# Linear attention and a highway layer on one core: half-height turns of k and q, row-halved scores and state, a compact state, and a new written order

## The chip, the core and the metric

The kernel runs on one core of a Trainium2 chip. The metric is the device time of one execution in microseconds. Three runs of the kernel before gave 109.04, 109.41 and 110.59; the median is 109.41.

## What is computed

First a decayed causal attention in blocks of 64 rows, with a 64 by 64 state for each batch and head; then a highway layer on the result.

```python
# q, k, v: (4, 8, 768, 64); lam: one decay for each of 8 heads
for b in range(768 // 64):
    intra = einsum('bhic,bhjc->bhij', qb, kb) * Dmask        # lam ** (i - j) for i >= j
    intra = einsum('bhij,bhjd->bhid', intra, vb)
    inter = einsum('bhid,bhde->bhie', qb * lam_pow, kv_state)
    out[:, :, sl] = intra + inter
    kv_state = lam_block * kv_state + einsum('bhsd,bhse->bhde', kb * rev_pow, vb)

x = out.transpose(0, 2, 1, 3).reshape(3072, 512)
H = maximum(x @ w_h, 0)
T = 1 / (1 + exp(-(x @ w_t + b_t)))
return T * H + (1 - T) * x                                   # (3072, 512), float32
```

## The kernel before

**Tiling.** The sequence is cut into twelve chunks of 256 rows, three for each batch, numbered n = 0 to 11. A chunk has two blocks b of 128 rows. Two consecutive rows lie in one partition (J = 2, the index j), so a load (`load`, line 170) moves runs of 512 bytes. The powers of the decay are put into q (`cast_q`, the factor `pow_q`) and v (`cast_v`, `pow_v`), both by `scale` (line 188), so that the mask is a triangle of ones and the state only adds up within a batch. k is only cast to bf16 (`cast_k`). Eight heads are four pairs hp of two heads e; in a transposed tile head e lies in the partitions `half(e)`.

**Stages of one chunk.** Tokens of the plan name them.

- `Lk Lq Lv`: loads of k, q and v, in halves of four heads (256 KB each), issued by SP. `CK CQ CV`: casts and scalings.
- `TK TQ`: transposes of k and q on PE (`trans`, line 199, into PSUM), eight 128x128 matmuls against the identity each. `EK EQ`: copies into `kT` and `qT` (lines 206 and 210).
- `SS.n.e` (`scores_state`, line 224): 16 score tiles of head half e (64 rows by 64 columns of the array, 128 columns moved), interleaved with 16 state tiles (64 columns moved) of block 1 - e. Scores of half e use the rows `half(e)` of the array, the states of block b the rows `half(b)`. The last chunk of a batch leaves out the state of block 1. Chunk 0 uses `S` and `U` instead.
- `KE` (`evac_s`, line 251): the PSUM state `kv` [128, 4, 128], which holds the two heads of a pair on its diagonal, is copied to `ss`. `M` (line 254): a mask of a PSUM bank of scores, 128x512, on DVE.
- `I` (`inter`, line 265): four 128x128 matmuls for a block, `ss` against `qT`. `A` (`intra`, line 276): 64x64 tiles, masked scores against `vs`, added in the same bank. `D` (`take`): copy to `xT`.
- `F.i.u.w` (`block`, line 295): eight matmuls of the highway layer for group i, column half u, weight w. `H` relu and subtraction on DVE (line 303), `G` two sigmoids on ACT (line 308), `X` the gate product (line 316), `R` (`turns`, line 340) the turn back, in half-height tiles of 64 rows against 64 columns of the identity, `E` its copy, `ST` the store by SP (512 KB). The last chunk is handled as two groups of 128 rows (11 and 12), with 128-column matmuls and stores in three parts.
- `W` loads a piece of the weights (512 KB, 256 rows of one matrix), `WC` casts a quarter matrix row block. `Z.r` runs r idle matmuls (`spin`) on PE.

**What sets the order.** The text `PLAN` (lines 17 to 60) is run from left to right (line 384). A token gives the operation, its indices, after `@` the engine, after `=` the PSUM banks (0 to 6; `kv` has one for itself). Each engine and each DMA queue works through its own instructions in this order; all large transfers are on SP's queue. SBUF buffers turn round in pools, five deep for the loads (`BUFS`, line 62).

Of the kernel before, what the change touches and what calls it, by code (L numbers as in the profile page):

```python
# [17 lines left out]
Lk.0.0 Lv.0.1 Lv.0.0 Lq.0.0 Lk.0.1 Lq.0.1 Lv.1.1 CK.0.0@POOL Lq.1.0 Z.12=0 TK.0.0=0 Lq.1.1 CV.0.0@DVE Lk.1.0  # L18
CQ.0.0@POOL EK.0.0@DVE Lv.1.0 CV.0.1@DVE CK.0.1@ACT Lk.1.1 Z.11=1 TQ.0.0=1 B=2 EQ.0.0@ACT CQ.0.1@POOL W.0.1 W.0.0
Z.6=0 TQ.0.1=3 TK.0.1=4 EQ.0.1@DVE U.0.0 EK.0.1@ACT W.1.1 S.0.0=56 KE.0.0@DVE S.0.1=01 CQ.1.2@POOL W.1.0 M.0.0.1 Z.1=3  # L20
U.0.1 I.0=34 M.0.1.1 KE.0.1@ACT Lk.2.1 M.0.0.0 A.0.1 M.0.1.0 TQ.1.2=0 Lq.2.1 CV.1.2@DVE CK.1.2@ACT EQ.1.2@ACT Lq.2.0
Z.8=1 TK.1.2=1 A.0.0 EK.1.2@DVE Lk.2.0 D.0.0@DVE Z.3=5 SS.1.1=56 WC.0.0.1@ACT WC.0.0.0@POOL M.1.1.0 KE.1.0@ACT
WC.0.1.0@POOL D.0.1@ACT Lv.2.1 WC.0.1.1@DVE Z.4=0 SS.1.0=01 M.1.1.1 I.1=35 KE.1.1@ACT Lv.2.0 F.0.0.0=4 WC.1.1.0@DVE PT
M.1.0.1 Lk.3.1 F.0.1.0=6 M.1.0.0 WC.1.0.0@POOL WC.1.0.1@ACT Lk.3.0 WC.1.1.1@DVE A.1.1 A.1.0 BC F.0.0.1=1 H.0.1 Lq.3.1
D.1.1@ACT H.0.0 D.1.0@ACT F.0.1.1=0 Lq.3.0 CQ.2.2@POOL F.1.0.0=2 Lv.3.0 G.0.1@ACT CK.2.2@DVE F.1.0.1=6 Lv.3.1
G.0.0@ACT X.0.1@DVE TQ.2.2=5 Lq.4.0 X.0.0@DVE TK.2.2=4 EQ.2.2@ACT CV.2.2@POOL F.1.1.0=3 Lq.4.1 EK.2.2@DVE G.1.0@ACT
H.1.0 SS.2.0=01 Lk.4.1 H.1.1 CK.3.2@POOL SS.2.1=54 Lk.4.0 M.2.0.1 F.1.1.1=2 KE.2.0@ACT M.2.1.0 Lv.4.0 TK.3.2=3 M.2.1.1
CQ.3.2@POOL G.1.1@ACT I.2=15 M.2.0.0 Lv.4.1 A.2.1 X.1.0@DVE A.2.0 Lk.5.0 R.0=40 D.2.0@ACT D.2.1@DVE CV.3.2@POOL
TQ.3.2=6 E.0.0@ACT Lk.5.1 F.2.1.1=1 E.0.1@ACT EQ.3.2@DVE Lq.5.1 EK.3.2@ACT X.1.1@DVE F.2.1.0=5 CQ.4.2@POOL Lq.5.0
R.1=40 H.2.1 SS.3.1=62 Lv.5.0 F.2.0.0=3 CK.4.2@POOL KE.3.0@ACT M.3.1.1 Lv.5.1 E.1.1@ACT M.3.1.0 SS.3.0=52 E.1.0@ACT  # L30
H.2.0 Lq.6.0 TQ.4.2=0 KE.3.1@ACT CV.4.2@POOL M.3.0.1 TK.4.2=6 G.2.1@ACT Lq.6.1 F.2.0.1=4 M.3.0.0 EQ.4.2@ACT EK.4.2@DVE
Lv.6.0 I.3=32 A.3.0 CK.5.2@POOL A.3.1 Lk.6.1 SS.4.1=56 D.3.0@ACT D.3.1@DVE TK.5.2=0 KE.4.0@ACT M.4.1.1 Lk.6.0
F.3.0.0=2 G.2.0@ACT CQ.5.2@POOL EK.5.2@DVE Lv.6.1 SS.4.0=36 H.3.0 F.3.0.1=0 Lq.8.0 M.4.0.0 CV.5.2@POOL M.4.0.1
TQ.5.2=2 Lk.9.0 G.3.0@ACT F.3.1.0=3 X.2.1@DVE Lq.7.0 EQ.5.2@ACT X.2.0@DVE F.3.1.1=6 CQ.6.2@POOL M.4.1.0 Lq.7.1
KE.4.1@ACT I.4=14 H.3.1 G.3.1@ACT R.2=25 Lk.8.1 X.3.0@DVE A.4.0 E.2.1@ACT X.3.1@DVE A.4.1 Lk.7.1 SS.5.0=30 E.2.0@ACT
D.4.0@DVE CK.6.2@POOL SS.5.1=56 D.4.1@ACT Lk.7.0 TQ.6.2=2 M.5.0.0 KE.5.0@ACT CV.6.2@POOL TK.6.2=1 M.5.1.1 Lv.7.0
EQ.6.2@ACT F.4.1.0=4 M.5.0.1 Lv.7.1 EK.6.2@ACT F.4.0.0=3 H.4.1 Lk.8.0 M.5.1.0 I.5=62 SS.6.1=01 H.4.0 Lq.8.1 A.5.0
KE.6.0@ACT M.6.1.0 CQ.7.2@POOL R.3=45 Lv.9.1 A.5.1 M.6.1.1 SS.6.0=30 D.5.0@ACT Lv.8.0 F.4.0.1=1 M.6.0.0 D.5.1@ACT
M.6.0.1 Lk.9.1 TQ.7.2=6 G.4.0@ACT CK.7.2@POOL F.5.0.0=3 Lq.10.1 EQ.7.2@ACT F.4.1.1=2 H.5.0 Lk.10.1 E.3.1@ACT X.4.0@DVE
TK.7.2=0 CV.7.2@POOL G.4.1@ACT I.6=63 ST.0 KE.6.1@DVE F.5.0.1=5 X.4.1@DVE Lv.8.1 F.5.1.0=1 G.5.0@ACT CK.8.2@POOL  # L40
EK.7.2@DVE Lq.9.0 A.6.0 E.3.0@ACT H.5.1 A.6.1 SS.7.1=20 Lq.9.1 D.6.0@ACT D.6.1@DVE TK.8.2=4 M.7.1.1 F.6.1.0=1 Lv.9.0
EK.8.2@ACT X.5.0@DVE CK.9.2@POOL F.6.1.1=6 KE.7.0@DVE Lk.10.0 CQ.8.2@POOL H.6.1 R.4=30 SS.7.0=54 Lk.11.1 E.4.0@ACT
F.5.1.1=1 E.4.1@ACT M.7.0.1 G.6.1@ACT ST.4 M.7.1.0 TK.9.2=3 Lq.10.0 M.7.0.0 TQ.8.2=0 G.5.1@ACT CV.8.2@POOL F.6.0.0=4
EQ.8.2@DVE Lk.11.0 KE.7.1@ACT X.5.1@DVE I.7=25 EK.9.2@ACT Lq.11.0 A.7.0 H.6.0 A.7.1 CQ.9.2@POOL SS.8.0=01 X.6.1@DVE
D.7.1@ACT Lv.10.1 SS.8.1=34 M.8.0.1 D.7.0@ACT F.6.0.1=6 KE.8.0@DVE Lq.11.1 CK.10.2@POOL F.7.0.0=5 M.8.1.0 G.6.0@ACT
M.8.1.1 ST.3 TQ.9.2=1 CV.9.2@POOL H.7.0 F.7.1.0=2 EQ.9.2@ACT Lv.10.0 X.6.0@DVE TK.10.2=3 M.8.0.0 ST.1 I.8=45
EK.10.2@ACT CQ.10.2@POOL H.7.1 SS.9.1=61 A.8.1 KE.9.0@ACT M.9.1.0 A.8.0 R.5=02 M.9.1.1 SS.9.0=36 CK.11.2@POOL
E.5.1@DVE F.7.0.1=1 KE.9.1@ACT M.9.0.1 E.5.0@ACT F.7.1.1=2 D.8.0@DVE D.8.1@ACT ST.5 CQ.11.2@POOL M.9.0.0 G.7.0@ACT
Lv.11.1 TK.11.2=6 Lv.11.0 I.9=04 F.8.1.0=5 EK.11.2@ACT ST.2 X.7.0@DVE TQ.10.2=3 G.7.1@ACT H.8.1 CV.10.2@POOL F.8.0.0=1
EQ.10.2@ACT R.6=65 H.8.0 A.9.1 X.7.1@DVE A.9.0 SS.10.1=31 D.9.0@ACT D.9.1@DVE F.8.1.1=2 E.6.1@ACT M.10.1.1 F.9.1.0=0  # L50
E.6.0@DVE G.8.1@ACT M.10.1.0 ST.6 TQ.11.2=4 CV.11.2@POOL KE.10.0@DVE F.9.1.1=5 EQ.11.2@ACT X.8.1@DVE SS.10.0=16
G.9.1@ACT H.9.1 R.7=32 M.10.0.1 KE.10.1@ACT F.8.0.1=4 X.9.1@DVE E.7.0@ACT M.10.0.0 E.7.1@ACT I.10=06 SS.11.0=53
G.8.0@ACT ST.7 A.10.0 M.11.0.0 A.10.1 SS.11.1=21 D.10.1@ACT X.8.0@DVE F.9.0.0=5 KE.11.0@ACT M.11.1.0 D.10.0@ACT
# [12 lines left out]
def kernel(  # L66
# [74 lines left out]
    kv = ps.tile([128, NP, 128], F32, tag="kv", name="kv", bufs=1)  # L141
# [4 lines left out]

    def groups(n, b):
        return ((n,), b) if n < N - 1 else ((n, b), 0)

    def new(key, shape, dtype=BF16, tag=None):  # L150
        if key not in made:
            tag = tag or key[0]
            made[key] = sb.tile(shape, dtype, tag=tag, name=tag, bufs=BUFS[tag])
        return made[key]

    def bank(key, i, shape, dtype=F32):
        if key not in made:
            made[key] = ps.tile(shape, dtype, tag=f"b{i}", name=f"b{key[0]}", bufs=1)
        return made[key]

    def get(*key):
        return made[key]
# [7 lines left out]
    def load(x, n, p, eng):  # L170
        b, c = divmod(n, NST)
        hs = heads(p)
        (A if eng else nc.sync).dma_start(out=new((x + "f", n), [128, H, J * D], F32)[:, hs],  # L173
                          in_=SRC[x][b, hs, c * 2 * C:(c + 1) * 2 * C, :].rearrange("h (p j) d -> p h (j d)", j=J))

    def load_w(w, g):
        nc.sync.dma_start(out=w_f[w][:, 2 * g:2 * g + 2],
                          in_=(moe_w_h, moe_w_t)[w][256 * g:256 * g + 256].rearrange("(kc p) m -> p kc m", p=128))

    def cast_w(w, g, i, eng):  # L180
        copy(eng, w_b[w][:, 2 * g + i], w_f[w][:, 2 * g + i])
# [17 lines left out]
    def trans(x, n, p, bk):  # L199
        hs = heads(p)  # L200
        t = bank((x + "tr", n, p), bk[0], [128, (hs.stop - hs.start) // 2, J, C], BF16)
        for i, h in enumerate(range(hs.start, hs.stop, 2)):
            for j in range(J):
                T.transpose(t[:, i, j, :], get(x + "b", n)[:, j, h:h + 2, :], id128)  # L204

    def evac_k(n, p, eng):
        hs = heads(p)
        copy(eng, new(("kT", n), [128, NP, J, C])[:, hs.start // 2:hs.stop // 2], get("ktr", n, p))

    def evac_q(n, p, eng):  # L210
        hs = heads(p)
        copy(eng, new(("qT", n), [128, NP, J, C])[:, hs.start // 2:hs.stop // 2], get("qtr", n, p))


    def score(n, e, hp, j, b):
        T.matmul(get("s", n, e, hp // 2)[half(b), hp % 2, j, :], lhsT=get("kT", n)[half(e), hp, j, half(b)],  # L216
                 rhs=get("qT", n)[half(e), hp, :, half(b)], start=True, stop=True)

    def state(n, b, hp, j, e):
        first = n % NST == 0 and b == 0 and hp == 0 and j == 0  # L220
        T.matmul(kv[half(e), hp, half(e)], lhsT=get("kb", n)[half(b), j, 2 * hp + e, :],  # L221
                 rhs=get("vs", n)[half(b), 2 * hp + e, j, :], start=first, stop=True, skip_group_check=True)

    def scores_state(n, e, bk):
# [194 lines left out]
```

## Time and profile before

| what | value |
|---|---|
| median of 3 runs | 109.41 us (109.04 to 110.59) |
| profiled execution, span of its instructions | 109.3 us; no other time is listed for it |
| granted TensorE clock, mean | 1.000 |
| bytes read, written in HBM | 20.98 MB, 6.29 MB |
| DMA, mean over the span | 252 GB/s |
| twelve loads each of k, q and v, in two halves | 24 issues of 256 KB each |
| DVE: masks (L255) | 48 of 0.682 us |
| ACT: copy of the state (L101), 128x512 | 15 of 0.595 us |
| DVE: gates (L318), 128x512 | 22 of 0.684 us |
| POOL: product of q and its powers (L190), 128x512 / 128x1024 | 2 of 1.310 us / 11 of 1.904 us |
| POOL: cast of k (L103), 128x1024 | 9 of 1.038 us |

Busy time counts a matmul from its start to its modelled end, and matmuls overlap in the array; so the durations of the groups are longer than the step from one matmul to the next. The chain of work that ended last shows the steps. In the rows of digits, each digit is the busy share of a fortieth of the span (2.73 us).

### The profile page before, as it was taken

The page shows a single profiled execution, that of the slowest core. Times are in us where ns is not written, and L with a number is a line of the kernel's source. Part 1 is how long each engine was busy: PE and PEld are TensorE (multiplying, and loading weights), DVE is VectorE, ACT ScalarE, POOL GpSimd, SP SyncE. Part 2 cuts the span into 40 slices and gives each one's busy share as a digit, 9 for nine tenths or more (in the row PEclk, how much of TensorE's full clock was granted, in tenths as well). Part 3 has the DMA queues.
Part 4 walks back from the last instruction along what each step waited for, and adds up shares of the span by engine and source line. Part 5 has one row for each costly group of instructions (what it writes and reads, how often), then busy time and mean ns, then how long its engine had stood idle before and what let it go on. Part 6 is the DMA issues. An engine that isn't in the chain of part 4 may idle for free.

```text
span 109.3 us, 4968 instructions
## 1 busy us (share of the span) xinstructions
PE 99.4 (91%) x2188; PEld 80.6 (74%) x2190; DVE 82.7 (76%) x140; ACT 71.9 (66%) x129; POOL 55.7 (51%) x46
## 2 busy tenths in 40 slices
PE   4986989899999999999999999998999599999950
PEld 1343654688887878889899889896888478899940
DVE  1241595878998696999977989999858958958960
ACT  3304263787866489499579749975696758776940
POOL 6029420427979858959468296499691600000000
PEclk9999999999999999999999999999999999999999
DMA  0899999999999999989999999599999413207264
GB/s 5 233 304 290 291 366 386 312 290 287 290 266 304 287 250 262 302 228 289 296 300 293 305 341 270 181 346 326 321 333 323 170 69 125 73 6 296 94 233 151
DMA packets 42701, 27.59 MB, mean 252 GB/s; under 512 B 1588, under 2 KB 38712, under 8 KB 42680
## 3 DMA queue, kind: packets, MB, share of 16 engines
q1 hardware_dynamic: 42528, 27.27, 85.1%
q8 instruction: 17, 0.28, 1.2%
q14 instruction: 4, 0.03, 0.1%
q10 hardware_dynamic: 152, 0.01, 0.1%
HBM read 20.98 MB, written 6.29 MB: 249 GB/s over the span
## 4 chain that ended last, share of the span: by engine, by line
PE 61%; DMA 11%; DVE 6%; POOL 5%; ACT 5%; issue 4%; SPq 4%; POOLq 0%; DVEq 0%
PE bt L300 15%; PE bh L300 13%; DMA qf<-in_q_dram 11%; PE bs L216 7%; PE bo L281 5%; PE bx L347 5%; PE bspin L366 4%; PE bqtr L204 4%; DVE m L255 3%; SPq L173 3%; PE bktr L204 3%; POOL qb L190 3%; PE bo L271 3%; ACT qT L101 2%; POOL vs L190 2%
## 5 line engine op out<-in xcount | busy, mean ns | idle before, releaser
L300 PEld LDWEIGHTS <-w_b 128*128 128x128 bf16 x416 | 36.3, 98 | 6.4 <-issue 1.8
L255 DVE TENSOR_TENSOR m<-bs,tri 128x512 bf16<-128x512 f32 x48 | 31.1, 682 | 3.8 <-PE bs L216 3.4
L190 POOL TENSOR_TENSOR qb<-qf,pow_q 128x1024 bf16<-128x1024 f32 (+1 forms) x13 | 23.6, 1813 | 11.2 <-DMA qf<-in_q_dram 10.6
L314 ACT ACTIVATE bt<-bt,bt_col 128x256 f32<-128x256 f32 (+1 forms) x52 | 22.0, 432 | 6.9 <-PE bt L300 4.2
L300 PE MATMUL bt<-xT,w_b 128*128 128x256 bf16 (+1 forms) x208 | 24.5, 265 | 1.3 <-ACT qT L101 1.3
L300 PE MATMUL bh<-xT,w_b 128*128 128x256 bf16 (+1 forms) x208 | 25.0, 265 | 0.2 <-issue 0.2
L190 POOL TENSOR_TENSOR vs<-vf,pow_v 128x1024 bf16<-128x1024 f32 x10 | 19.0, 1904 | 5.0 <-DMA vf<-in_v_dram 4.6
L305 DVE SCALAR_TENSOR_TENSOR hm<-bh,xT 128x512 bf16<-128x512 f32 (+1 forms) x26 | 16.5, 643 | 4.0 <-PE bh L300 2.5
L318 DVE TENSOR_TENSOR th<-bt,hm 128x512 bf16<-128x512 f32 (+1 forms) x26 | 16.5, 643 | 2.1 <-ACT bt L314 2.0
L216 PE MATMUL bs<-qT,kT 64*64 64x128 bf16 x384 | 14.2, 218 | 0.6 <-issue 0.3
L101 ACT ACTIVATE xT<-bo 128x512 bf16<-128x512 f32 x16 | 11.5, 749 | 4.6 <-PE bo L281 4.6
L103 POOL CAST kb<-kf 128x1024 bf16<-128x1024 f32 (+1 forms) x10 | 10.0, 995 | 8.1 <-DMA kf<-in_k_dram 6.8
L101 ACT ACTIVATE ss<-kv 128x512 bf16<-128x512 f32 x15 | 8.9, 595 | 7.3 <-PE bs L216 6.1
L366 PE MATMUL bspin<-blank,id 128*128 128x512 bf16 x43 | 11.8, 416 | 1.6 <-POOL id masks.py:199 1.4
L216 PEld LDWEIGHTS <-kT 64*64 64x64 bf16 x384 | 11.0, 106 | 2.9 <-issue 1.4
L101 ACT ACTIVATE o<-bx 128x512 f32<-128x512 f32 x19 | 10.4, 596 | 1.4 <-PE bx L347 1.3
L101 ACT ACTIVATE qT<-bqtr 128x1024 bf16<-128x1024 bf16 (+1 forms) x10 | 9.8, 980 | 1.8 <-PE bqtr L204 1.8
L281 PE MATMUL bo<-m,vs 64*64 64x128 bf16 x384 | 9.4, 219 | 0.7 <-DVE m L255 0.4
L221 PE MATMUL kv<-vs,kb 64*64 64x64 bf16 x320 | 9.2, 196 | 0.2 <-POOL vs L190 0.2
L366 PEld LDWEIGHTS <-id 128*128 128x128 bf16 x45 | 4.3, 105 | 6.4 <-issue 1.7
L204 PE MATMUL bqtr<-id,qb 128*128 128x128 bf16 x96 | 7.5, 220 | 0.9 <-POOL qb L190 0.9
L281 PEld LDWEIGHTS <-vs 64*64 64x64 bf16 x384 | 6.6, 106 | 2.4 <-issue 1.5
(50 smaller groups left out, 109.1 us busy)
## 6 DMA issues: line engine op xcount, KB each, us to landing
kf<-in_k_dram SPq DMA_DIRECT2D x24, 256.0 KB, 5.5
vf<-in_v_dram SPq DMA_DIRECT2D x24, 256.0 KB, 5.4
qf<-in_q_dram SPq DMA_DIRECT2D x24, 256.0 KB, 5.5
out_dram<-o SPq DMA_DIRECT2D x11, 512.0 KB, 4.7
w_f<-in_moe_w_h_dram SPq DMA_DIRECT2D x2, 512.0 KB, 6.6
w_f<-in_moe_w_t_dram SPq DMA_DIRECT2D x2, 512.0 KB, 8.5
out_dram<-oh SPq DMA_DIRECT2D x2, 128.0 KB, 2.0
out_dram<-oq SPq DMA_DIRECT2D x1, 256.0 KB
```

The costliest lines, as they stand in the source:

```text
L101: A.activation(dst, src, AF.Copy)
L103: ENG[eng].tensor_copy(dst, src)
L190: ENG[eng].tensor_tensor(dst, in0=get(src, n)[:, heads(p)].rearrange("p h (j d) -> p h j d", j=J), in1=pw[:, n % NST, heads(p), :, None].t ...
L204: T.transpose(t[:, i, j, :], get(x + "b", n)[:, j, h:h + 2, :], id128)
L216: T.matmul(get("s", n, e, hp // 2)[half(b), hp % 2, j, :], lhsT=get("kT", n)[half(e), hp, j, half(b)], rhs=get("qT", n)[half(e), hp, :, ha ...
L255: V.tensor_tensor(new(("m", n, e, u), [128, 2, J, C]), in0=get("s", n, e, u), in1=tri[:, None].to_broadcast([128, 2, J, C]), op=ALU.mult)
L281: T.matmul(get("o", n, b)[half(e), hp, :], lhsT=get("vs", n)[half(b), 2 * hp + e, j, :], rhs=get("m", n, e, u)[half(b), hp % 2, j, :], sta ...
L300: T.matmul(t[:, r, :], lhsT=w_b[w][:, kc, (2 * u + r) * 128:(2 * u + r + 1) * 128], rhs=get("xT", *g)[:, kc, :], start=(kc == 0), stop=(kc ...
L305: V.scalar_tensor_tensor(new(("hm", g, u), [128, 2, z * C], tag=f"hm{z}"), in0=get("h", g, u), scalar=0.0, in1=get("xT", *g)[:, 2 * u:2 * ...
L314: A.activation(dst[:, r, :], src[:, r, :], AF.Sigmoid, bias=bt_col[:, 2 * u + r:2 * u + r + 1])
L318: ENG[eng].tensor_tensor(new(("th", g), [128, NP, z * C], tag=f"th{z}")[:, 2 * u:2 * u + 2, :], in0=get("tt", g, u), in1=get("hm", g, u), ...
L366: T.matmul(t, lhsT=id128, rhs=blank, start=True, stop=True)
```

## The change

The diff changes these things together.

- *Turns of k and q together* (`trans_both`, `evac_both`, tokens `T` and `ET`, chunks 2 to 11): instead of 16 transposes of 128x128, 32 of a row half against 64 columns of the identity; half r of the rows goes to the bank `tr` r, k and q side by side. One copy for each bank writes both into one tile `kq`. Chunks 0 and 1 keep `TK` and `TQ`.
- *Scores and state in equal row halves* (`tiles`, `scores_state_a`, `scores_state_b`, tokens `SA` and `SB`): SA does the state of block 0 and the first scores of half 0 on one row half, all scores of half 1 on the other; SB the rest of the scores of half 0 beside the state of block 1. `tiles` interleaves the two lists in pairs by the numbers 56 and 32 given for a pair.
- *Compact state*: `kv` and `ss` are [128, 4, 64], without the empty squares beside the diagonal.
- *Inter*: for a block eight 64 by 64 tiles (row half e to column half e), in a call for each block. Both row halves write the same bank.
- *Gates*: nine of 26 (u = 1 of groups 2 to 10) go from DVE to POOL; their sigmoids are written to an SBUF tile `tb` in float32.
- *Weights* are loaded and cast in halves of their columns instead of their rows.
- *Order and buffers*: a new plan. Buffers are named in it (`slots`) instead of turning round. Idle matmuls are 34 instead of 45. The weights are loaded after three chunks instead of two; `ST.2`, `ST.1`, `ST.3` and `ST.6` stand ahead of the last load, where `ST.0`, `ST.4`, `ST.3`, `ST.1` and `ST.5` did.
- Copies by engine, before and after: turned k and q in whole copies ACT 15 to 11, DVE 7 to 9; `KE` ACT 15 to 16, DVE 5 to 4; `D` ACT 16 to 14, DVE 8 to 10; `E` of whole chunks ACT 19 to 15, DVE 3 to 7.

```diff
 PLAN = """
-Lk.0.0 Lv.0.1 Lv.0.0 Lq.0.0 Lk.0.1 Lq.0.1 Lv.1.1 CK.0.0@POOL Lq.1.0 Z.12=0 TK.0.0=0 Lq.1.1 CV.0.0@DVE Lk.1.0
...
-ST.11.0.2 E.11.1.0@DVE ST.11.1.0
+Lk.0.1=0 CK.0.1@POOL=0 Lq.1.0=0 CQ.1.0@DVE=0 Lq.0.0=1 B=0 Lk.0.0 CQ.0.0@DVE=1 Z.19=2 TK.0.1=1 Z.7=3 TQ.0.0=2 Lq.0.1
...
+ET.2.0@DVE Z.2=1 I.2.0=2 W.1.0 D.1.1@DVE=1 WC.1.0.1@DVE WC.1.0.0@ACT W.0.0 SA.2=140 M.2.0.0=1 KE.2.0@ACT=0 M.2.1.0=2
+M.2.1.1=0 F.0.0.1=6 WC.0.0.1@POOL I.2.1=5 SB.2=1 WC.0.0.0@ACT F.0.0.0=4 G.0.0 W.0.1 WC.0.1.1@ACT M.2.0.1=3 A.2.1 W.1.1
+D.1.0@DVE A.2.0 F.1.0.1=0 Lq.3.0=3 F.1.0.0=1 Lk.3.0=3 Lq.3.1 WC.1.1.0@DVE D.2.1@ACT=2 D.2.0@ACT WC.0.1.0@DVE F.0.1.0=3
...
+E.7.1@ACT=2 E.7.0@ACT T.11=32 ET.11.1@ACT=2 Lv.11.0 ST.7 ET.11.0@DVE I.10.1=5 I.10.0=6 SB.10=4 F.9.1.1=0 G.9.1=1
+M.10.0.1=3 CV.11.2@POOL=3 A.10.1 A.10.0 KE.10.1@DVE=3 ST.5 SA.11=132 M.11.0.0=5 M.11.1.1=7 I.11.0=4 D.10.0@ACT=0
+KE.11.0@ACT=1 D.10.1@DVE F.9.1.0=0 H.9.1=2 F.8.0.1=6 X.9.1@POOL I.11.1=1 X.8.1@POOL=1 SB.11=2 M.11.0.1=4 ST.4
...
+E.11.1.0@DVE=1 ST.11.1.0
 """
...
+POOL_GATES = [(2, 1), (3, 1), (4, 1), (5, 1), (6, 1), (7, 1), (8, 1), (9, 1), (10, 1)]
...
-    kv = ps.tile([128, NP, 128], F32, tag="kv", name="kv", bufs=1)
+    kv = ps.tile([128, NP, 64], F32, tag="kv", name="kv", bufs=1)
...
-        nc.sync.dma_start(out=w_f[w][:, 2 * g:2 * g + 2],
-                          in_=(moe_w_h, moe_w_t)[w][256 * g:256 * g + 256].rearrange("(kc p) m -> p kc m", p=128))
+        nc.sync.dma_start(out=w_f[w][:, :, 256 * g:256 * g + 256],
+                          in_=(moe_w_h, moe_w_t)[w][:, 256 * g:256 * g + 256].rearrange("(kc p) m -> p kc m", p=128))
...
+    def trans_both(n):
+        for r in range(2):
+            bank(("tr", n, r), [128, 2, NP, J, 64], BF16)
+        for i, x in enumerate("kq"):
+            for hp in range(NP):
+                for j in range(J):
+                    for r in range(2):
+                        T.transpose(get("tr", n, r)[:, i, hp, j, :], get(x + "b", n)[half(r), j, 2 * hp:2 * hp + 2, :], id128[half(r), half(r)])
+
+    def evac_both(n, r, eng):
+        copy(eng, kq(n)[:, :, :, :, half(r)], get("tr", n, r))
...
-        T.matmul(kv[half(e), hp, half(e)], lhsT=get("kb", n)[half(b), j, 2 * hp + e, :],
+        T.matmul(kv[half(e), hp, :], lhsT=get("kb", n)[half(b), j, 2 * hp + e, :],
...
+    def tiles(*rows):
+
+        todo = sorted((sum(w for w, _ in row[:i]), r, i) for r, row in enumerate(rows) for i in range(len(row)))
+        for _, r, i in todo:
+            for go in rows[r][i][1]:
+                go()
+
+    def score_pairs(n, e, hps):
+        return [(56, [lambda hp=hp, j=j, b=b: score(n, e, hp, j, b) for b in range(2)]) for hp in hps for j in range(J)]
+
+    def state_pairs(n, b):
+        return [(32, [lambda hp=hp, j=j, e=e: state(n, b, hp, j, e) for e in range(2)]) for hp in range(NP) for j in range(J)]
+
+    def scores_state_a(n):
+        for e, u in ((0, 0), (1, 0), (1, 1)):
+            bank(("s", n, e, u), [128, 2, J, C])
+        tiles(state_pairs(n, 0) + score_pairs(n, 0, (0, 1)), score_pairs(n, 1, range(NP)))
+
+    def scores_state_b(n):
+        bank(("s", n, 0, 1), [128, 2, J, C])
+        tiles(score_pairs(n, 0, (2, 3)), [] if n % NST == NST - 1 else state_pairs(n, 1))
...
-        copy(eng, new(("ss", n + b, 1 - b), [128, NP, 128]), kv)
+        copy(eng, new(("ss", n + b, 1 - b), [128, NP, 64]), kv)
...
+    def inter(n, b):
+        for hp in range(NP):
+            for e in range(2):
+                T.matmul(out_bank(n, b)[half(e), hp, :], lhsT=get("ss", n, b)[half(e), hp, :],
+                         rhs=kq(n)[half(e), 1, hp, :, half(b)], start=o_first(n, b, e), stop=False, skip_group_check=True)
...
-                    T.matmul(get("o", n, b)[:, hp, :], lhsT=get("ss", n, b)[:, hp, :],
-                             rhs=get("qT", n)[:, hp, :, half(b)],
-                             start=hp == 0, stop=False, skip_group_check=True)
...
+        made["tt", g, u] = new(("tb", g, u), [128, len(rows(g, u)), size(g) * C], F32) if (g, u) in POOL_GATES else t
```

## The prediction

> **What bounds the kernel now.** I read the page's head first, then the chain that ended last in order of time, then the groups by shape, then the timelines of POOL at both ends of the run.
>
> ```profile
> span 109.3 us, 4968 instructions
> PE 99.4 (91%) x2188; PEld 80.6 (74%) x2190; DVE 82.7 (76%) x140; ACT 71.9 (66%) x129; POOL 55.7 (51%) x46
> PEclk9999999999999999999999999999999999999999
> DMA  0899999999999999989999999599999413207264
> ```
>
> PE and DMA are both full until about 84 us, at full clock all along; DMA then empties while PE goes on. The chain shows what PE really costs, since it counts one matmul from its start to the next one's:
>
> ```profile
> 22.09 1.75 PE bh L300 x16
> ...
> 37.12 0.15 PE bs L216 x2
> ...
> 37.53 0.17 PE bs L216 x6
> 37.69 0.98 PE bh L300 x8
> ...
> 79.67 0.22 PE bo L271 x4
> 79.89 0.87 PE bh L300 x8
> 80.77 0.45 PE bqtr L204 x8
> ...
> 82.46 0.57 PE bx L347 x32
> 83.03 0.57 PE bo L281 x32
> ...
> 91.22 0.45 PE bs L216 x12
> ...
> 101.84 0.45 PE bh L300 x8
> ```
>
> The reader is to see prices: an FFN block of eight 256-column matmuls 0.87 us, of 128 columns 0.45; eight 128x128 transposes 0.45 (0.056 each); four inter matmuls 0.22; 32 half-height turns (L347) 0.57; 32 intra tiles (L281) 0.57; one scores-and-state call (16 + 16 tiles, from 37.12 to 37.69) 0.57, but 16 scores alone (91.22) 0.45. Three different mixes of 32 small tiles take 0.57: a small tile costs 0.0178 us whatever its columns, unless only two of the four quarters of the array work, when a pair of 128-column tiles costs 0.056.
>
> ```profile
> 5.32 0.61 POOL L103 CAST kb<-kf 128x512 bf16<-128x512 f32 x1 [2.64 <-DMA kf<-in_k_dram]
> ...
> 84.88 1.90 POOL L190 TENSOR_TENSOR vs<-vf,pow_v 128x1024 bf16<-128x1024 f32 x1 [2.42 <-DMA vf<-in_v_dram]
> ```
>
> The first load is used at 5.32, the last at 84.88. ACT's timeline has the twelfth load used at 15.19, so (15.19 - 5.32)/11 = 0.90 us a load of 256 KB.
>
> The PE ledger of before: the FFN starts at 22.1 and its last block ends at 104.2 (PE's timeline). In between lie 44 x 0.87 + 8 x 0.45 = 42.0 of FFN; 11 output turns x 0.57 = 6.3; 20 transpose calls (chunks 2 to 11) x 0.45 = 9.0; 20 scores-and-state calls x 0.57, less 0.12 for the four without states, = 10.9; 17 inter x 0.22 = 3.8; 11 intra x 0.57 = 6.3. Sum 78.3 of 82.1 us; 3.8 us are stalls. After 104.2 come 5.1 us of last gate, turn, copy and store.
>
> **The change, part by part.** I put the same ledger on the new order.
>
> *Start.* Three chunks (18 loads) go ahead of the weights now, two before. At 0.90 a load the 18th is used at 5.32 + 17 x 0.90 = 20.6; V's scaling on POOL (1.90) ends at 22.5, the first scores-and-state call of chunk 2 (40 tiles x 0.0178 = 0.71) at 23.3. The first weight piece, two loads' bytes, is there at 22.4 and cast (0.6) by 23.0, so the FFN starts at 23.3, 1.2 later, but with chunk 2's transposes, first scores and half its inter done. The fourth piece lands at 5.32 + 25 x 0.90 = 27.8, cast at 28.4, and is wanted at about 28.7: no stall, with 0.3 to spare. Spins fall from 45 to 34; they lie in idle time before 22 us, so nothing is gained.
>
> *Transposes of k and q together.* 32 half-height tiles for 16 full ones: 0.57 by L347, whose tile shape it is, against 0.90; the pair unable to overlap gives 0.90 again. I take 0.57: 9 chunks x 0.57 = 5.1 (bounds 5.1 to 8.1). The Trainium skill (TensorE: Matmul & The Clock Gate, "Wait — 56ns, not 53.3ns?") says starts never come closer than about 25 ns; by it the call would be 0.80, and the ledger 2.1 us longer. L347's 17.8 ns contradicts it, so the sum goes by the row.
>
> *Scores and state in row halves.* SA is 40 tiles, SB 24 (8 without state). By the tile price 0.71 + 0.43 = 1.14, exactly the two calls of before; only the four chunks without state gain (0.71 + 0.22 against 1.02). Chunks 3 to 11 and SB.2: 9 x 0.71 + 6 x 0.43 + 4 x 0.22 = 9.9. The even split buys almost nothing.
>
> *Inter as 64 by 64.* Eight tiles where four stood. If both diagonal quarters run together it is four pairs x 0.056 = 0.22 as before; if not, 0.45. No row shows two row halves writing one PSUM bank at once: L281, L347 and L216 write a different bank from each half. I take 0.22, nearest L281's tiles: 16 x 0.22 = 3.6 (bounds 3.6 to 7.2). The Trainium skill (TensorEngine Tiling, Gotcha 1: PSUM Pressure) says that different row tiles cannot access one bank at the same time; by it the dear end holds, and the time is 3.6 more.
>
> *Compact state.* The copies read 256 columns instead of 512. ACT's 128x256 (0.449) is the nearest row, 0.34 and 0.595 the bounds: about 16 x 0.15 = 2.4 us less on ACT.
>
> *Gates on POOL.* Nine of 0.684 leave DVE (6.2 us). POOL's 128x512 products took 1.04 and 1.58; I take 1.1. POOL per chunk: 1.90 + 1.04 + 1.90 + 1.1 = 5.9, below PE's 6.7 (four FFN blocks, two turns, 1.07 of scores and state, 0.4 of inter, 0.57 of intra). A gate waits for ACT's sigmoids, and the next chunk's k, q and v casts stand behind it.
>
> *Copies of the turns.* ACT loses 15 whole copies for 11 (1.03 each); DVE has 9 for 7, plus two more `take`s (0.73) and four more output copies (0.69). The new destination has runs of 64: DVE's contiguous COPY is 0.69, its one strided cast of this size 1.63; I take 0.69, as both rows of copies of a whole PSUM bank show. DVE's chunk is then four masks and two relus at 0.68, one gate, 0.6 of `take`, 0.6 of turn copies, 0.55 of the rest: 6.5, just below PE's 6.7, as it was before (6.8 against 7.1); that closeness is why I keep the stalls of before. At 1.63 it would be 7.3, and nine chunks 5.4 longer: 110.2.
>
> *Order and queues.* SP has four big stores ahead of the last load instead of five; one is 0.52 MB, 1.8 us at the 290 GB/s of the middle slices. So the last load is used near 83.1. Weight pieces keep their bytes. The stores moved behind it (3.7 MB) take 13 us of the 20 left; covered.
>
> *Sum.* FFN 42.0, turns out 6.3, transposes 5.1, scores and state 9.9, inter 3.6, intra 10 x 0.57 = 5.7: 72.6. From 23.3, with the same 3.8 of stalls and the same 5.1 at the end: 104.8. By the loads: 83.1 + 1.9 for V, then everything from SA.11 on (0.71 + 0.45 + 0.22 + 0.57 + 7 x 0.87 + 8 x 0.45 + 3 x 0.57 = 13.4), its share of stalls 0.6, and 5.1: 104.1. Both limits meet; the later is 104.8. The profiled execution's 109.3 stands 0.1 below the median of the runs, 109.41, so nothing is corrected.
>
> **The rivals.** *Inter tiles take turns at the bank.* For it: no row shows the overlap. Against: the halves write different partitions, as L281's columns do. 104.8 + 3.6 = 108.4: no change.
>
> *Loads come no earlier.* DMA is full in before; if the pace, not the store in front, sets the last load, V is ready at 86.8 and the end is 105.9; if the late weights and gates on POOL cost it 2 more, 107.9: no change.
>
> *The state copy becomes a wait, and the time rises.* SB writes the bank that the first state copy reads, and half of inter needs that copy. Before, PE never idled for the state (inter's idle is 0.0). Now between SA and the work that needs it lie only one FFN block or an intra call in many chunks (0.57 to 0.87), and the copy (0.45) may stand behind two sigmoids (0.9) on ACT. If 0.6 us stays uncovered in each of 12 chunks, 7.2 us: 112.0, slower. It decides from about 0.57 a chunk; below 0.2 it is within the forecast.
>
> *The stalls of before go.* If 2 of the 3.8 vanish, and loads keep up: 102.8.
>
> **How the numbers follow.** Forecast with both limits near 104.8 (own range 103 to 106.8): 0.50. Stalls gone, 101.5 to 103: 0.10. Bank turns or late loads, 107.2 to 110: 0.23. State wait or DVE bound, over 111.6: 0.13; between 110 and 111.6: 0.04. A change of 2% is about what a measurement of this kernel tells from none; 2% below the median is 107.2, above it 111.6. Faster 0.61, same 0.25, slower 0.14. Range 102.0 to 110.5: it leaves out the slow end and a little below.
>
> **What would show it.** The chain or timeline of the changed kernel should have 32 transposes in 0.57, 40 tiles of SA in 0.71, eight inter tiles in 0.22 (0.45 is the bank rival), the FFN beginning near 23.3, the last V used near 83, the last FFN block ending near 99.7. A PE wait for ss, or DVE copies over 1 us, would make it wrong upwards. SA in 0.48 would mean that the floor is not one of tiles, and the time 2 to 3 us less.

## The result and the profile after

The changed kernel took 121.41 us (median of 4 runs, 121.20 to 122.33); the kernel before, beside it on the same chip, 109.36 (109.04 to 110.59). The ratio is 1.111, with a 95% interval of 1.104 to 1.119: 12 us slower, where 104.8 was forecast. The profiled execution took 121.2 us with a span of 119.2, so about 2.0 us lie outside the span. Some executions of these kernels ran 1 to 2% longer than the others; the ratios leave them out, the medians and some of the profiles do not, and the ratios are what I compare.

The head of the page of after (rows of 40 slices of 2.98 us), its row of instruction packets, and the shares of the chain that ended last:

```profile
span 119.2 us, 5435 instructions
...
PE 97.4 (82%) x2419; PEld 76.0 (64%) x2419; DVE 83.0 (70%) x139; ACT 63.6 (53%) x125; POOL 66.0 (55%) x56
...
PE   0299969366799998399697999894999999999960
...
PEclk9999999968999999999999999998599999999999
DMA  0999999999998999977991019999990806803964
...
q8 instruction: 19, 0.31, 1.2%
...
PE 75%; issue 11%; DVE 5%; ACT 3%; DMA 3%; DVEq 0%
```

PE is busy for 2.0 us less than before, in a span 9.9 us longer: the time is idle PE. Of the other engines only POOL's share rose, from 51% to 55%, which doesn't explain it. "issue" (the engine, here nearly always PE, waits for nothing that the profile shows) is 11% of the chain, where before it was 4%. PEclk has a 6 and a 5, where before it was full throughout. The lines that I had not weighed in before were these two:

```profile
q8 instruction: 17, 0.28, 1.2%
...
PE 61%; DMA 11%; DVE 6%; POOL 5%; ACT 5%; issue 4%; SPq 4%; POOLq 0%; DVEq 0%
```

Queue 8 brings pages of instructions: 17 packets before and 19 after, 0.31 MB / 19 = 16 KB each.

The chain of after, at the start:

```profile
5.00 0.28 DVE kv L160
...
5.32 0.23 PE bbt L395
5.55 6.80 PE bspin L401 x19
12.36 0.22 PE bktr L225 x4
12.58 1.51 PE bspin L401 x7
...
14.96 0.51 ACT L416
15.48 0.78 issue
...
17.89 0.42 PE bs L245 x16
...
34.08 1.03 PE bt L339 x8
```

Two lines of the timelines of PE and POOL go with it:

```profile
20.73 1.90 POOL L208 TENSOR_TENSOR vs<-vf,pow_v 128x1024 bf16<-128x1024 f32 x1 [0.54 <-DMA vf<-in_v_dram]
...
30.78 1.05 PE L339 MATMUL bt<-xT,w_b 128*128 128x256 bf16 x8
```

The bias transpose (`B=0`, tile bbt) stands in front of the idle matmuls now, and waits until 5.3 us. Nineteen idle matmuls (tile bspin) behind it take 6.80 us: they start 0.43 us apart until 10.6 and 0.216 apart from 10.9 on, as the next seven do. By PE's timeline the first scores come at 16.9 (12.2 before), and the first FFN block began at 30.78 (23.3 forecast; 21.9 before). But V of chunk 2 was scaled on POOL from 20.73 to 22.63: the loads came as forecast, PE did not.

The same chain further on:

```profile
20.62 0.22 PE bo L303 x8
...
22.29 0.35 PE bo L303 x6
22.64 2.19 issue
...
28.89 1.59 issue
...
39.48 0.57 PE btr L238 x32
...
46.75 0.61 PE bt L339 x4
47.36 2.13 issue
49.49 0.61 PE bt L339 x4
...
57.63 0.54 PE bh L339 x4
58.18 0.97 issue
59.14 0.61 PE bh L339 x4
...
80.07 0.42 PE btr L238 x28
80.49 1.65 issue
82.14 0.23 PE btr L238 x4
82.37 1.71 PE bt L339 x8
```

The prices hold: eight inter tiles 0.22, 32 half turns 0.57. But blocks are torn apart in their middle, where all operands are there: an FFN block stands still for 2.13 us between its fourth and fifth matmul. After the gap at 80.5 an FFN block takes 1.71 instead of 0.87: PEclk's 5. The granted clock was 0.5 for 3.41 us from 24.4 and from 82.5 us.

The groups by shape give the copies and gates of after:

```profile
L119 ACT ACTIVATE ss<-kv 128x256 bf16<-128x256 f32 x16 | 6.3, 391 | 7.2 <-PE kv L250 7.2
L121 DVE COPY kq<-btr 128x1024 bf16<-128x1024 bf16 x9 | 6.1, 681 | 1.4 <-PE btr L238 1.4
L353 POOL TENSOR_TENSOR th<-tb,hm 128x512 bf16<-128x512 f32 x9 | 10.4, 1156 | 20.1 <-PE bx L383 5.2 <-ACT bt L350 4.5 <-PE bt L339 3.4
```

0.391, 0.681 and 1.156 against 0.449, 0.69 and 1.1 taken.

**Where the gaps stand.** I numbered PE's matmuls in the trace by their start. Counted from 0, the big gaps come after matmuls 222, 350, 734, 990, 1118, 1502, 1630 and 2142: all 94 more than a multiple of 128. A matmul and its weight load are two instructions, so the gaps stand at multiples of 256 PE instructions, and a 16 KB packet of queue 8 would hold 256 instructions of 64 bytes. Not every page end has a gap. I call the 128 matmuls between two such places a page. Idle PE at page ends (the steps over 0.25 us there, less 0.06 each, from 14 us on) sums to 2.6 us before and 11.75 after; 4.1 of the 11.75 (at 24.84 and 30.49) stand ahead of the first FFN block, 7.65 behind its start.

### The profile page after: what moved, and what is told of

Same layout as the page of the kernel before. It is cut to its first block, busy times and chain, and to the rows that moved or that the text cites. A ratio compares the mean times of both kernels' runs of the same rounds, so it can differ in the third digit from the quotient of the medians.

```text
span 119.2 us, 5435 instructions
## 1 busy us (share of the span) xinstructions
PE 97.4 (82%) x2419; PEld 76.0 (64%) x2419; DVE 83.0 (70%) x139; ACT 63.6 (53%) x125; POOL 66.0 (55%) x56
## 4 chain that ended last, share of the span: by engine, by line
PE 75%; issue 11%; DVE 5%; ACT 3%; DMA 3%; DVEq 0%
PE bt L339 19%; PE bh L339 18%; PE bspin L401 8%; PE bo L313 7%; PE bs L245 6%; PE bx L383 5%; PE bo L303 5%; PE btr L238 4%; DMA lam_bc<-in_lam_dram 3%; PE kv L250 2%; DVE m L287 2%; ACT kq L119 2%; DVE th L353 1%; DVE hm L343 1%; DVE xT L121 1%
## 5 line engine op out<-in xcount | busy, mean ns | idle before, releaser
L287 DVE TENSOR_TENSOR m<-bs,tri 128x512 bf16<-128x512 f32 x48 | 31.0, 683 | 10.9 <-PE bs L245 6.8
L208 POOL TENSOR_TENSOR vs<-vf,pow_v 128x1024 bf16<-128x1024 f32 (+1 forms) x13 | 22.7, 1751 | 7.6 <-DMA vf<-in_v_dram 7.6
L353 POOL TENSOR_TENSOR th<-tb,hm 128x512 bf16<-128x512 f32 x9 | 10.4, 1156 | 20.1 <-PE bx L383 5.2
L350 ACT ACTIVATE bt<-bt,bt_col 128x256 f32<-128x256 f32 (+1 forms) x34 | 14.4, 425 | 9.6 <-PE bt L339 9.0
L245 PE MATMUL bs<-kq 64*64 64x128 bf16 x384 | 15.9, 227 | 3.8 <-issue 2.8
L119 ACT ACTIVATE kq<-btr 128x1024 bf16<-128x1024 bf16 x11 | 11.3, 1028 | 10.9 <-PE btr L238 10.9
L245 PEld LDWEIGHTS <-kq 64*64 64x64 bf16 x384 | 11.5, 111 | 4.6 <-issue 4.1
L121 POOL CAST kb<-kf 128x1024 bf16<-128x1024 f32 (+1 forms) x11 | 10.5, 958 | 6.0 <-DMA kf<-in_k_dram 5.5
L353 DVE TENSOR_TENSOR th<-bt,hm 128x512 bf16<-128x512 f32 (+1 forms) x17 | 10.5, 625 | 3.0 <-ACT bt L350 2.0
L250 PE MATMUL kv<-vs,kb 64*64 64x64 bf16 x320 | 10.5, 200 | 0.3 <-DVE vs L208 0.3
L303 PE MATMUL bo<-kq,ss 64*64 64x128 bf16 x160 | 7.8, 221 | 2.8 <-issue 2.2
L119 ACT ACTIVATE ss<-kv 128x256 bf16<-128x256 f32 x16 | 6.3, 391 | 7.2 <-PE kv L250 7.2
L350 ACT ACTIVATE tb<-bt,bt_col 128x256 f32<-128x256 f32 x18 | 7.6, 475 | 3.8 <-PE bt L339 3.8
L250 PEld LDWEIGHTS <-kb 64*64 64x64 bf16 x320 | 8.5, 113 | 1.2 <-issue 1.1
```

Of the source, the lines that this page charges most:

```text
L119: A.activation(dst, src, AF.Copy)
L121: ENG[eng].tensor_copy(dst, src)
L208: ENG[eng].tensor_tensor(dst, in0=get(src, n)[:, heads(p)].rearrange("p h (j d) -> p h j d", j=J), in1=pw[:, n % NST, heads(p), :, None].t ...
L250: T.matmul(kv[half(e), hp, :], lhsT=get("kb", n)[half(b), j, 2 * hp + e, :], rhs=get("vs", n)[half(b), 2 * hp + e, j, :], start=first, sto ...
L287: V.tensor_tensor(new(("m", n, e, u), [128, 2, J, C]), in0=get("s", n, e, u), in1=tri[:, None].to_broadcast([128, 2, J, C]), op=ALU.mult)
L303: T.matmul(out_bank(n, b)[half(e), hp, :], lhsT=get("ss", n, b)[half(e), hp, :], rhs=kq(n)[half(e), 1, hp, :, half(b)], start=o_first(n, b ...
```

## The experiments

The theory: (1) the start is late because the bias transpose holds the idle matmuls and all transposes behind it; (2) a page of PE instructions is fetched by DMA about one page ahead, and arrives late when 128 matmuls go by in 3 to 4 us while data transfers fill the queues; many small tiles make pages short. Rivals: PE waits for buffers or engines in the new order; the loads; the half clock as a cause of its own.

**The bias transpose later.**

```diff
-... Lq.0.0=1 B=0 Lk.0.0 CQ.0.0@DVE=1 Z.19=2 TK.0.1=1 Z.7=3 TQ.0.0=2 Lq.0.1
+... Lq.0.0=1 Lk.0.0 CQ.0.0@DVE=1 Z.19=2 TK.0.1=1 Z.7=3 B=0 TQ.0.0=2 Lq.0.1
```

> The bias turn goes behind the first spins, nothing else. Start theory (the bias waits for its load until 5.3 us, so the spins begin cold and late and hold up the first transposes): the spins begin near 1.5, the first score tiles at 12.5 to 13.5 instead of 16.9, the FFN 3 to 4 us earlier, the time near 118. Page theory (PE stands still at every 128th matmul when a 16 KB packet of instructions comes late; in the changed kernel 12 us): the early waits are made up while V of chunk 2 is awaited, the page gaps stay, and the time falls by less than 1.5 us, 120 to 121.5.

114.89 us (113.43 to 115.67), ratio 1.045 [1.035, 1.055]. The idle matmuls start at 1.43, the first scores at 12.48 (4.4 earlier) and the FFN at 25.35 (5.4 earlier). The chain of this run goes through the loads at the start, as the forecast had it:

```profile
13.32 6.86 DMA kf<-in_k_dram
```

So the token held up the start of this kernel. The gain was larger than either theory had said (118, or 120 to 121.5): 0.066 of the ratio, 7.2 us. The gaps at page ends nearly stayed (10.9 us), but 1.9 of them stand ahead of the first FFN block now, where 4.1 did, and the clock fell to 0.5 once, at 22.0, where it had fallen twice. So the 7.2 us are not the token's wait alone.

**Full transposes again** (chunks 2 to 11: eight 128x128 matmuls each for k and q, whole copies), the rest as in the changed kernel.

```diff
-T.2=06 ET.2.1@ACT=2 ... ET.2.0@DVE
+TK.2.2=0 TQ.2.2=6 EQ.2.2@ACT=2 ... EK.2.2@DVE
```

> Chunks 2 to 11 turn k and q in 16 full transposes again instead of 32 half ones. By tile prices alone PE has 10 x 0.33 = 3.3 us more: 124.7. Page theory: PE has 320 fewer instructions (1.25 pages) and the same pages last longer, so the gaps at the page ends fall from 12 us to 6 to 9: 119 to 122, not above 122.

115.81 us (114.77 to 117.38), ratio 1.054 [1.045, 1.064]. By the prices this edit costs 10 x (0.90 - 0.57) = 3.3 us; it gained 0.057 of the ratio, 6.2 us, more than expected. PE has 160 matmuls less and 17 pages instead of 19, and the gaps at page ends fell from 11.75 to 4.6 us, further than the 6 to 9 expected. In this execution the 19 idle matmuls also took 5.59 us instead of 6.80, which is not of the edit's making. And most of the gain lies at the start: the FFN began at 25.56 instead of 30.78, although the bias transpose still stood in front. From the first FFN block to the last this kernel took 82.0 us, the changed one 83.2: there the shorter gaps outweigh the 3.3 us by about 1 us.

**No late loads.** Loads of chunks 5 to 11 are left out, and their buffers hold an earlier chunk's rows; everything else is issued as before.

```diff
     def load(x, n, p):
...
+        if (x + "f", n) not in made and n >= 5:
+            made[x + "f", n] = made[last[x, slots.pop(0)]]
+        if n >= 5:
+            return
```

> The loads of chunks 5 to 11 are left out; those chunks read the buffers of earlier ones, so the output is not the reference's. PE's instructions are the same. Page theory with a full DMA queue as the reason for late pages: the gaps after 40 us (about 7.6 us, and the half clock after the one at 80) shrink to under 0.3 us each, time 111 to 113. If the gaps come from dependencies on PE's inputs from ACT and DVE, or if a page is late whatever else the DMA does, they stay and the time is above 118.

114.41 us (114.02 and 114.80), ratio 1.045 [1.034, 1.055]. DMA carries next to nothing but stores from 37 us on, and PE runs the same instructions. Its chain, at the two blocks that were torn in after (the FFN's line is L347 in this file):

```profile
48.35 1.06 PE bt L347 x8
...
56.94 0.98 PE bh L347 x8
```

Whole blocks, no gap. The page ends side by side, from the two traces (columns: the time that the page before took; from its first matmul to the start of the 16 KB packet that comes next; the step at the page end, 0.11 being an FFN matmul's own):

| matmul of after | after: page, packet, step (us) | no late loads: page, packet, step |
|---|---|---|
| 734 | 2.99, 2.80, **2.41** | 3.00, 0.47, 0.11 |
| 990 | 3.33, 2.16, **1.24** | 3.33, 0.01, 0.11 |
| 1118 | 3.60, 1.66, **0.95** | 3.61, 0.06, 0.03 |
| 1374 | 4.69, 0.55, 0.03 | 4.69, 0.09, 0.03 |
| 1502 | 3.73, 1.80, **0.67** | 3.75, 2.07, **0.72** |
| 1630 | 3.26, 2.78, **1.84** | 3.26, 1.09, **0.47** |
| 2142 | 3.34, 1.14, **0.67** | 3.31, 0.48, 0.11 |

The pages take the same time; what differs is when the packet starts. Where there is a gap, PE goes on 2.3 to 2.9 us after that start (packets last 0.9 to 2.0). So the step is about the packet's delay plus 2.6, less the page's time: 2.80 + 2.6 - 2.99 = 2.41. Without loads most packets of the table start within 0.5 us. At 1502 stores fill DMA; at 1630 the packet started 1.09 late though DMA moved nothing in that time, and why is open. So two gaps stayed above the 0.3 expected. Behind 40 us the gaps sum to 1.1 us, where after has 7.65; from the first FFN block to the last it is 5.0 us less. The time is above the 111 to 113 expected: loads are still there ahead of 37 us, and so is a step of 2.93 at a page end, to 28.77. That is the page theory as I would now state it, and loads matter by their traffic, not by their arrival.

**64 matmuls more at the very start**, one column each, into a bank of their own:

```diff
+    slots[:] = [3]
+    few = bank(("few",), [128, 1])
+    for _ in range(64):
+        T.matmul(few, lhsT=id128, rhs=blank[:, 0:1], start=True, stop=True)
     for token in PLAN.split():
```

> 64 one-column matmuls are added at the very start, where PE is idle until 5.3 us. Page theory: every gap over 0.3 us after 18 us lies 64 matmuls earlier in the work than a page end of before, at the new numbers 94 + 128 k; those at matmuls 222, 350 and 734 of the changed kernel vanish and others appear; their sum may be anything from 6 to 14 us, time 115 to 124. Dependency theory: the gaps stay at the same work, 64 numbers later, and the time stays within 1 us of 121.4.

116.78 us (116.18 and 117.38), ratio 1.066 [1.055, 1.078]. More work, and 0.045 of the ratio less. Chain:

```profile
57.38 0.54 PE bt L339 x4
57.92 1.01 issue
58.93 0.61 PE bt L339 x4
...
78.88 2.26 issue
...
85.50 0.29 PE bx L383 x20
85.79 1.27 issue
87.06 0.35 PE bx L383 x12
```

By the new count the gaps stand again at one place modulo 128 (91 or 92; a few records are missing), which is 64 matmuls earlier in the work: other blocks are torn, one of them an output turn that ran whole before. A wait for a buffer or an engine would have stayed with its instruction. The gaps sum to 9.1 instead of 11.75, since other stretches of work now make up the pages; this run's idle matmuls, which ended 0.8 us earlier than in after, help as well. So where the page ends fall in the work is alone worth up to 4.9 us here, and a single edit that moves them is not to be priced by one run.

**Undoing more, in steps.** First the bias later and full transposes together:

> Both edits at once: bias turn behind the first spins, and full transposes in chunks 2 to 11. Alone they gave 6.5 and 5.6 us; 1.2 of the second was a shorter run of spins, which the first takes away anyway. Page theory: 121.4 - 6.5 - 4.4 = 110.5 (109.5 to 112), page gaps after 18 us 3 to 6 us. If half transposes were not what filled the pages, the second edit costs its 3.3 us of PE time: 118.

112.25 us (110.99 to 113.07), ratio 1.023 [1.017, 1.030], just above the 109.5 to 112 expected. Gaps at page ends 5.1 us. The FFN began at 25.40, no earlier than with full transposes alone (25.56) or the bias alone (25.35): at the start the two edits gain the same time, not each its own.

Then the wide state and four full inter matmuls in addition:

```diff
-    kv = ps.tile([128, NP, 64], F32, tag="kv", name="kv", bufs=1)
+    kv = ps.tile([128, NP, 128], F32, tag="kv", name="kv", bufs=1)
...
-            for e in range(2):
-                T.matmul(out_bank(n, b)[half(e), hp, :], lhsT=get("ss", n, b)[half(e), hp, :],
+            T.matmul(out_bank(n, b)[:, hp, :], lhsT=get("ss", n, b)[:, hp, :],
```

> Also the state as [128, 4, 128] and inter as four full matmuls again, so PE has 160 instructions less and the state copies 0.2 us more each on ACT. By tile prices PE's time is unchanged. Page theory: the gaps shrink a little further, 0.5 to 2 us less than the kernel with both other edits. If ACT's copies matter, 1 to 3 us more than it.

111.46 us (109.62 to 111.85), ratio 1.014 [1.004, 1.023], gaps 2.1 us.

The same wide state with the half turns kept and the bias later:

> Bias turn behind the first spins, wide state and full inter, half transposes kept: 160 PE instructions fewer than with the bias edit alone, PE's time by tile prices unchanged. Page theory: page gaps 1 to 3 us less, 112 to 114. If the tiles of inter were slowed by sharing a bank, the gain would be 3.6 us or more, with the gaps unchanged.

112.26 us (111.98 to 113.34), ratio 1.033 [1.027, 1.039], gaps 6.5 us. Beside the bias alone (1.045) the wide state gains 0.012, 1.3 us: four matmuls in 0.22 for eight in 0.22, that is, fewer instructions for the same time. The two intervals overlap, so the gain in time is likely and not shown; the gaps fell by 4.4 us, from 10.9, more than the 1 to 3 expected. Beside the run with full transposes (1.014), the half turns cost 0.019 here, 2.1 us; beside each other, the bias alone (1.045) and bias with full transposes (1.023) give 0.022, 2.3 us. With the 6.2 above that makes three pairs: in this kernel the half turns, cheap by themselves, cost 2 to 6 us more than they save.

**ACT's table load just before the copy of the bias** (`PT`, 1.28 us), in front of the first state copy of chunk 1, instead of between the copies of the first two chunks; the rest as in the kernel with full transposes and the wide state (1.014):

> As before it, with ACT's second table load (1.28 us) behind the copies of the first two chunks instead of between them. Start theory: the first score tiles come about 1 us earlier; 0.3 to 1 us less. If V of chunk 2 decides the start, no change.

111.09 us (109.14 to 112.39, 10 runs), ratio 1.007 [1.002, 1.013]. No gap at page ends over 0.25 us, and still no faster than the kernel before. PE's timeline shows why:

```profile
19.11 0.40 PE L301 MATMUL bo<-kq,ss 128*128 128x128 bf16 x4 [1.92 <-ACT ss L118]
...
21.38 1.03 PE L224 MATMUL bktr<-id,kb 128*128 128x128 bf16 x8 [1.50 <-POOL kb L120]
```

PE now waits for that state copy, then for k of chunk 2, and the granted clock is 0.5 for 6.83 us from 20.2. The table load was put in a bad place.

**The table load behind that copy, and five idle matmuls** in front of the transposes of k of chunk 2 (beside the kernel with full transposes and the wide state; `PT` is gone from its old place):

```diff
-... KE.1.0@ACT=2 I.1.1=5 SB.1=1 TK.2.2=0 TQ.2.2=6 ...
+... KE.1.0@ACT=2 PT I.1.1=5 SB.1=1 Z.5=0 TK.2.2=0 TQ.2.2=6 ...
```

> This is the kernel with B=0 later, full transposes, wide state and four full inter matmuls (111.46 us), with the load of ACT's table set behind the first state copy of chunk 1 and five more idle matmuls in front of the transposes of k of chunk 2. In the kernel with the table load just before BC, PE waited 1.92 us for that state copy (it stood behind the table load), 1.50 us for the cast of chunk 2's k, and then ran 6.8 us at half clock. Theory (the remaining loss against the kernel before is a late start plus half clock after these waits): the wait for ss goes, the half-clock window shrinks to 3.4 us or none; 108.0 to 110.0. Rival (the loss sits elsewhere, in the order after 30 us): 111 to 111.5. A clock below 0.9 in no digit with a time still over 110.5 would speak for the rival.

109.60 us (109.02 to 111.53, 10 runs) against 109.66 for the kernel before on this chip, ratio 1.000 [0.996, 1.004]. The FFN starts at 24.38, gaps 0.5 us, and the page of this kernel shows

```profile
span 107.1 us, 4962 instructions
...
PE   4999496699999999999999999999999999999930
...
PEclk9999999999999999999999999999999999999999
...
q8 instruction: 17, 0.28, 1.1%
```

full clock again. What is left of the change here (row halves of scores and state, gates on POOL, weights after three chunks, the new order), with five idle matmuls more and the table load moved, gives together no difference that could be measured. No kernel beat the one before.

**The start theory on the kernel before.** `B=2` in front of `Z.12`, nothing else:

> The kernel before with one token moved: the bias transpose B=2 in front of the first idle matmuls (Z.12), as the changed kernel has it. Start theory: the idle matmuls begin near 5.3 us instead of 1.43, run at half clock until about 9 us, push the first transposes and the first scores back by 2 to 4 us, and the FFN starts at 23.5 to 26 instead of 22: 110.5 to 113.5. Rival (idle matmuls lie in idle time, as the prediction had it; the loads set the start): 108.9 to 109.5, FFN start unchanged.

111.79 us (111.12 to 112.88), ratio 1.019 [1.010, 1.028]. PE's timeline:

```profile
5.54 0.23 PE L360 MATMUL bbt<-id_f,bt_r 4*128 4x4 f32 x1 [5.54 <-DMA bt_r<-in_moe_b_t_dram]
5.71 4.97 PE L366 MATMUL bspin<-blank,id 128*128 128x512 bf16 x12
```

The FFN starts at 25.54 instead of 21.92: 3.6 us later, though PE had been "idle" before it. The time rises by 2.1 only, and the gaps at page ends fall from 2.6 to 0.3 us.

**A dose of small tiles and a dose of large ones**, in the kernel before. Small: 24 of the 32 score tiles of chunks 2 to 10 are done twice.

```diff
-            score(n, e, hp, j, x)
+            for _ in range(2 if 2 <= n <= 10 and i < 12 else 1):
+                score(n, e, hp, j, x)
```

> The kernel before, with 24 of the 32 score tiles of chunks 2 to 10 done twice: 216 small tiles more, 216 x 0.0178 = 3.84 us by the price of a tile. Page theory (every 128 matmuls a new page of instructions is fetched, and it is late when the last 128 went by quickly while DMA is full): the tiles also bring 1.7 more pages and shorter ones, the gaps at page ends rise from 2.6 to 5 to 8 us: 114 to 118 us, at least 2 us more than the dose of large matmuls beside it. Price theory alone: 112 to 113, as the large dose.

Large: the first matmul of each FFN block of groups 2 to 10 is done twice.

```diff
+        if 2 <= i <= 10:
+            T.matmul(t[:, 0, :], lhsT=w_b[w][:, 0, 2 * u * 128:(2 * u + 1) * 128],
+                     rhs=get("xT", *g)[:, 0, :], start=True, stop=True)
```

> The control to the small dose: the kernel before with one 256-column matmul more in each of the 36 FFN blocks of groups 2 to 10 (the first one done twice): 36 x 0.109 = 3.92 us of PE, but only 36 instruction pairs. Page theory: pages last longer, gaps at page ends 1 to 3 us as before, 112 to 113.2. Price theory alone: the same 112 to 113 as the small dose. Less than 111 would say that PE's own work has slack in it.

Small: 117.62 us (116.75 to 118.64), ratio 1.072 [1.062, 1.082]. Large: 114.02 (113.55 to 114.37), ratio 1.041 [1.034, 1.048]. The difference is 0.031, 3.3 us, for PE work that I had priced alike. But the small dose was dearer than priced: calls of scores and state without a gap went from 0.57 to about 0.91, probably because a doubled tile falls on the same quarter of the array; 18 x 0.34 = 6.1 us, not 3.84. So 2.2 us of the 3.3 are my wrong price. The gaps at page ends are 3.9 us against 1.7. That is the sense that the page theory wants, but less than the 5 to 8 expected, and 2.2 us of gaps are more than the 1.1 left to explain; the large dose, too, lies above the 112 to 113.2 expected. The chain of the small dose has its second largest gap inside such a call:

```profile
52.86 0.16 PE bs L216 x6
53.02 1.38 issue
54.40 0.21 PE bs L216
```

The page before it took 2.68 us; the largest, a step of 1.65 us from 83.3 on, came after 2.29. These are the two shortest pages of that kernel. This pair supports the theory, but doesn't prove it alone.

## Why the prediction was wrong

By its own steps, on spans: 104.8 forecast, 119.2 measured. The start is 30.78 - 23.3 = 7.5 of it; from there to the last FFN block (about 113.9 instead of 99.7) 6.7; the tail 0.2.

- **Start, failed.** "Spins fall from 45 to 34; they lie in idle time before 22 us, so nothing is gained", and an FFN at 23.3, set by the loads. The loads did as worked out (V ready at 22.63, forecast 22.5). I had walked the loads, POOL and SP through the new order, and not PE's own queue: `B=0` is ahead of `Z.19`, and waits until 5.3. The idle matmuls were not idle time but time in front of the first transposes. Moving that token brought the FFN forward by 5.4 us and gave back 0.066 of the ratio, 7.2 us; on the kernel before, where hardly a gap stands at the start, the mirrored move put the FFN back by 3.6 and cost 2.1. The token is not all of the 7.5: the gaps of 4.1 us and the half clock from 24.4 stand in the same stretch, and with full transposes the FFN began at 25.56 with the token in its place. How the 7.5 divide stays open. No variant of the changed kernel reached the forecast 23.3; the earliest began at 24.38.
- **"With the same 3.8 of stalls", failed.** I tied the stalls to DVE being nearly as full as PE. They are of another kind: gaps at page ends, 2.6 us before and 11.75 after, 7.65 of them behind 30.78. The half turns and the inter tiles put more instructions into the same time, so pages grow shorter than the fetch. The half clock after the gap at 80.5 adds about 1.5 us (FFN block 1.71 for 0.87, 16 intra tiles and a scores call likewise). 7.65 + 1.5 leaves 1.4 of the 10.5 us of stalls (3.8 + 6.7) for all else.
- **Prices, right.** Half turns 0.57 (32 starts in it, 17.8 ns each), inter 0.22, the turn's copy 0.681, the POOL gate 1.156, the state copy 0.391. The ledger of 72.6 stood: the stretch from 30.78 to 113.93, less the gaps and the half clock, is 74.0. It was a sum of busy work, and the loss was between the work.
- **Last load, wrong without effect.** V of chunk 11 was used at 97.68, not near 83: between 70 and 100 us SP waited 22.0 us for output copies in front of its stores. PE did not wait for it.
- **Rivals.** The bank turns of inter are refuted: two row halves wrote one bank at 0.22 for eight tiles, so the rule of the Trainium skill that was weighed there (TensorEngine Tiling, Gotcha 1) did not bind. The wait for the state copy, my way to "slower", is refuted too (PE waited 0.6 us for ss in all). Stalls that go: the opposite came. The sign "slower" came true by two mechanisms that I had not named.
- **The reference.** I set the span 109.3 beside the median 109.41 and corrected nothing. About 2.0 us lie outside a span, so that execution was some 2 us slower than the median. Forecast and reference were both spans, so this cancels in the forecast change of 4.5; of the 16.6 us between 104.8 and the median of 121.41, 14.4 are accounted for above, and 2.2 lie outside the span.

What each undone step was worth, by the ratios: bias later 7.2 us, full transposes 2.3, wide state 1.0, table load and clock 1.5: 12.0 of the 12.1. The intervals on both sides of the first two steps do not meet, those of the last only just, and those of the wide state overlap; the whole is what is sure. They are in this order, and another order shares them otherwise: with full transposes first, those are worth 6.2 us and the bias 3.4.

## What to carry to other kernels

Halving the time of a PE operation by doubling its instructions pays only while 128 matmuls last longer than the fetch of the next 128: here pages of 2.3 to 5.6 us came late with DMA full; with DMA quiet, pages of 2.9 to 3.3 us came in time, but for one. Gaps marked "issue" inside a block, at equal distances in the count of matmuls, are the sign. And when an order is rewritten, walk each engine's queue from its first instruction: what stands in front of "idle" warm-up work decides when the real work begins.

## What the runs showed of the hardware that was not expected

- **Pages of instructions.** The Trainium skill (Runtime: NRT & Kernel Launch, "Instruction fetch mechanics") says that instructions are refilled in 16 KiB blocks, and that the crossing is mostly hidden. The 16 KB packets, one for each 128 matmuls with their loads, agree. Hidden they are not here: up to 2.41 us at one crossing and 11.75 in a run. The packet starts 0.0 to 1.1 us after the crossing into the page before when DMA moves next to nothing (no late loads, from 45 us on), and up to 4.9 us with DMA full; after a gap PE goes on 2.3 to 2.9 us after it starts (changed kernel and no late loads), elsewhere it was more (3.5 in the run with 64 matmuls more, where the packet itself took 2.04).
- **The clock.** The granted clock fell to 0.5 for 3.41 us after stretches with PE gaps of 1.8 to 2.4 us (24.4 and 82.5 us in after), and in the run with the table load before the copy of the bias for 6.83 us from 20.2, after a wait of 1.9 us and across one of 1.5. Steps of 1.81 and 2.41 us at page ends of after (to 30.49 and 49.49) were not followed by a fall. What exactly sets it off was not tried.
- **Idle matmuls at the start.** The same 19 took 6.80, 5.59 and 5.55 us in different executions (changed kernel, full transposes, no late loads). The page's PEclk shows 9 all through them, but their steps show half speed: 0.43 us each at first, then 0.216, and the trace has its first entry of full clock only at 10.8, 8.3 and 8.4 us. From the first idle matmul to that entry it was 2.6 us in the kernel before, 5.3 in the changed one and 5.8 with bias and full transposes together; so over 1 us of the start varies by itself. The Trainium skill (TensorE: Matmul & The Clock Gate, "What's actually happening") says that the gate's window of 3413 ns is free-running, so that the moment of full speed varies, by 500 ns to either side; the 3.41 us above agree, and the spread in these runs is larger.
